# An attention and gated-MLP kernel: two more accumulator banks for the MLP

## The chip, the cores and the metric

The kernel runs on one core of a Trainium2 chip. The metric is the device time of one execution in microseconds (us); the time before is a median of three timed runs, and one further execution was profiled.

## The reference, cut to what matters

There are 8 batches, 8 heads, 576 tokens and a head dimension of 64; the model dimension is 512, the hidden one 1024.

```python
def _attn_ref(q, k, v, f):
    scores = scale * np.matmul(q, k.transpose(0, 1, 3, 2))
    cum = np.cumsum(np.log(np.clip(f, 0.0001, 1.0)), axis=-1)
    scores = np.where(causal, -1e9, scores + cum[..., :, None] - cum[..., None, :])
    attn = softmax(scores)                       # row by row
    return np.matmul(attn, v)

def _moe_ref(x, w_in, w_spatial, b_spatial, w_out):   # x: attention's output, heads side by side
    h = np.maximum(x @ w_in, 0.0)
    u, v = h[..., :512], h[..., 512:]
    v_n = (v - mean(v)) / np.sqrt(var(v) + 1e-6)      # over the 512 columns
    v_s = np.einsum('ts,bsd->btd', w_spatial, v_n) + b_spatial[None, :, None]
    return (u * v_s) @ w_out
```

## The kernel before, in words

Heads are worked on in pairs, four pairs to a batch, 32 in all. The kernel interleaves two streams. `attention(b)` works through the four pairs of batch b. `moe(b)` is the gated MLP of batch b and needs the x tiles (xh and xl, a value and its rest) of all four pairs. The driving loop writes down `moe(b)` piece by piece, and between its pieces `attention(b + 1)` in proportion.

Attention, per pair: scores of four row blocks on TensorE into score banks "sc" (L326, the last 64 rows through L233 with qk_t as input), VectorE adds the decay and takes the lowest value (L306, out nm), ScalarE takes the exponential (L337, L375), GpSimd divides by the sum (L314). From pair 8 on (the third batch; `moved`) the weights are turned without TensorE: VectorE transposes blocks of 32 into the buffer mid (L456), and 16 transfers in SyncE's queue bring them to e (L463). The product with v follows (L488, L493, in score banks too), and ScalarE and VectorE split the result into xh (L510) and xl (L513). For pairs 0 to 7 the transposes are TensorE's, into the banks of the pool "t", tag "tp" (L414, L425, L405).

The MLP, per batch: five v tiles of 128 tokens (12 matmuls of 512 columns each, 8 for the last), read out by ScalarE at L773 into vx, of which there are two, or for the last by L771 and L772; normalised (L774 to L778), split into vnh and vnl (L780, L782). Eight u tiles (12 matmuls of 256 or 320 columns), read out by ScalarE (L801). Then for each of the two halves of the tokens four spatial tiles (14 matmuls), multiplied into u by VectorE (L823), split into gh (L826, ScalarE) and gl (L827, GpSimd), and two output tiles (12 matmuls of 512 columns), read out by ScalarE (L851) and sent to DRAM. Every odd batch has one more output tile, with the last 64 tokens of two batches.

Each of these tiles gets its accumulator from `acc(b)`. The 8 PSUM banks of 2 KB are four of tags sc0 to sc3, two of tag tp, and two of the pool `ps_m` (tag ps). Before, batches 0 to 6 take theirs from `ps_m` alone, two in turn; the last batch, after which there is no more attention to write down, takes from `ps_m`, from tp and from the score banks in turn. A tile can be written again once its former content has been read.

The order of the instructions on each engine is fixed when the program is built. A planner runs a time model of the engines, and whenever one is free it places the instruction written earliest among those whose inputs and buffers it holds ready. At run time each engine keeps to that order and waits where an input or a buffer isn't ready. So a change of buffers can change the order on every engine.

Of the kernel before, what the change touches and what calls it, by code (L numbers as in the profile page):

```python
# [38 lines left out]
def attn_gmlp_kernel(ctx: ExitStack, tc: tile.TileContext, qk, v, f, w_in, w_sp, b_sp, w_out, out):  # L39
# [7 lines left out]
    B = out.shape[0]  # L47
# [687 lines left out]
    nps = [0]  # L735

    def acc(b):

        nps[0] += 1
        k = nps[0] % 3 if b == B - 1 else 0  # L740
        pool, tag = ((ps_m, "ps"), (PS["t"], "tp"), (PS["s"], f"sc{nps[0] // 3 % 4}"))[k]
        return pool.tile([128, DM], F32, name=tag)

    def moe(b):
        X = [xs.pop(b * PPB + p) for p in range(PPB)]
        vh, vl = [], []
        for i in range(NB + 1):
            for n in (2 * i, 2 * i + 1) if b == 0 and i < NB else ():
                load_rest(n, win_v, winh, winl, ("exp", PPB - 1, 1, 0))
            ps = acc(b)  # L750
            n = 0
            for p in range(PPB):
# [37 lines left out]
        for j in range(NJ):  # L790
            for t0, nt in HALVES:
                ps = acc(b)
                n = 0
                for p in range(PPB):
                    xh, xl = X[p]
                    for l, r in ((winh, xh), (winl, xh), (winh, xl)):
                        mm(ps[:, 0:nt], l[:, p, 128 * j:128 * j + 128], r[:, t0:t0 + nt], n == 0, n == 3 * PPB - 1)
                        n += 1
                    yield 369
                us[j, t0] = mo.tile([128, 320], F32, name="u", tag="U", bufs=9)  # L800
                A.activation(us[j, t0][:, 0:nt], ps[:, 0:nt], AF.Relu)  # L801
# [6 lines left out]
        for t0, nt in HALVES:  # L808
            gh, gl = [], []
            for j in range(NJ):  # L810
                ps = acc(b)
                o = ps[:, 0:nt]
                js = slice(128 * j, 128 * j + 128)
                for c in range(NB):
                    mm(o, vh[c][:, js], sph[:, c, t0:t0 + nt], c == 0, False)
                    mm(o, vh[c][:, js], spl[:, c, t0:t0 + nt], False, False)
                    mm(o, vl[c][:, js], sph[:, c, t0:t0 + nt], False, False)
                    yield 370
                mm(o, vh[NB][:, js], spta[:, t0:t0 + nt], False, False)
                mm(o, vb_[:, js], sptb[:, t0:t0 + nt], False, True)  # L820
                yield 246
                g = us[j, t0][:, 0:nt]
                V.tensor_tensor(out=g, in0=o, in1=g, op=ALU.mult)  # L823
                gh.append(mo.tile([128, 320], F32R, name="gh", tag="GH", bufs=3))
                gl.append(mo.tile([128, 320], F32R, name="gl", tag="U", bufs=9))
                A.copy(gh[j][:, 0:nt], g)  # L826
                G.tensor_tensor(out=gl[j][:, 0:nt], in0=g, in1=f32(gh[j][:, 0:nt]), op=ALU.subtract)  # L827
                if t0:
                    for r, gg in enumerate((gh[j], gl[j])):
                        V.tensor_copy(gt[0][r][:, j, r0:r0 + 64], f32(gg[:, 256:320]))  # L830
            for c0 in (0, 128):
                yield from w_out_tile(b, [g[:, c0:c0 + 128] for g in gh], [g[:, c0:c0 + 128] for g in gl],
                                      [(b, t0 + c0, 0, 128)])
# [92 lines left out]
```

## Time and profile before

| what | value |
|---|---|
| median of three timed runs | 747.42 us (747.03 to 747.93) |
| profiled execution | 752.48 us |
| its span, first to last instruction | 750.3 us |
| TensorE busy | 700.4 us, 93% |
| VectorE, GpSimd, ScalarE busy | 64%, 51%, 49% |
| granted TensorE clock, mean | 0.979 |

The span is what the rows count from. The granted clock is the share of TensorE's full clock that the chip let through. PE is TensorE, PEld its weight loads, DVE VectorE, ACT ScalarE, POOL GpSimd, SPq SyncE's queue. A row of the timeline gives start, length, engine, line, operation, output and inputs, shape, and in brackets how long the engine had been idle and what ended that.

### The profile page before, as it was taken

To read this page: it belongs to the slowest core of one execution; us is meant where nothing else is said; L and a number is where in the kernel's file an instruction comes from. 1 tells how busy PE (TensorE), PEld (TensorE's weight loads), DVE (VectorE), ACT (ScalarE), POOL (GpSimd) and SP (SyncE) were. 2 spreads that over 40 slices of the span, in tenths; PEclk is the share of its full clock that TensorE was granted. 3 is DMA by queue.
4 is the path that set the end of the run, shared out by engine and by line. 5 is a ranking of instruction groups with operands and counts; after the bars stand their busy time and mean duration, and the time that the engine had idled before them with its cause. 6 is when DMAs were issued, how large, how long until landed. Compare 5 with 4: busy or idle time off the path is not lost.

```text
span 750.3 us, 14594 instructions
## 1 busy us (share of the span) xinstructions
PE 700.4 (93%) x4709; PEld 554.1 (74%) x4709; DVE 480.3 (64%) x1597; ACT 369.2 (49%) x1028; POOL 380.1 (51%) x703
## 2 busy tenths in 40 slices
PE   7878979789989898999999999999999999999997
PEld 3545757558778586797778777788779787899886
DVE  6787787855676575667666766767666766821332
ACT  6866586663544344645444444544454435521231
POOL 3887555584554453544475454635464455611241
PEclk9999999999999899999999999999999999999999
DMA  7855344246657777557874687657965686330001
GB/s 234 240 151 144 108 145 133 78 127 184 191 160 188 194 188 206 155 147 204 213 204 136 179 220 226 178 114 203 227 172 151 176 226 178 84 88 29 29 1 70
DMA packets 52749, 117.82 MB, mean 157 GB/s; under 512 B 10305, under 2 KB 14401, under 8 KB 52674
## 3 DMA queue, kind: packets, MB, share of 16 engines
q1 hardware_dynamic: 48082, 108.64, 53.7%
q10 hardware_dynamic: 4592, 8.26, 3.2%
q8 instruction: 37, 0.61, 0.4%
q14 instruction: 38, 0.31, 0.2%
HBM read 67.78 MB, written 9.75 MB: 103 GB/s over the span
## 4 chain that ended last, share of the span: by engine, by line
PE 52%; DVE 8%; POOL 8%; ACT 6%; issue 5%; DMA 2%; SPq 2%; ACTq 0%; POOLq 0%; DVEq 0%
PE ps L233 34%; PE sc L326 6%; PE sc L488 5%; POOL tt L314 4%; PE sc L233 3%; ACT tt L337 3%; DMA e<-mid 2%; PE tp L233 2%; DVE mid L456 2%; SPq L463 1%; PE sc L493 1%; DVE tt L306 1%; POOL vnl L782 1%; DVE st L774 1%; ACT o L851 1%
## 5 line engine op out<-in xcount | busy, mean ns | idle before, releaser
L337 ACT ACTIVATE tt<-tt,nm 128x384 f32<-128x384 f32 (+2 forms) x240 | 132.7, 554 | 69.0 <-DVE nm L306 66.4
L314 POOL TENSOR_SCALAR tt<-tt,sm 128x128 f32<-128x128 f32 x208 | 110.0, 549 | 49.3 <-DVE sm L353 47.0
L456 DVE STREAM_TRANSPOSE mid<-tt 128x128 f32<-128x128 f32 x192 | 90.7, 494 | 30.7 <-POOL tt L314 26.1
L827 POOL TENSOR_TENSOR gl<-u,gh 128x256 fp32r<-128x256 f32 (+1 forms) x64 | 51.4, 805 | 100.7 <-ACT gh L826 99.6
L326 PE MATMUL sc<-qk_t 64*128 64x128 f32 (+3 forms) x512 | 90.3, 473 | 9.2 <-DVE nm L306 4.8
L233 PE MATMUL ps<-xh,winh 128*128 128x256 f32 (+1 forms) x232 | 71.8, 312 | 4.2 <-DVE vx L772 2.8
L233 PE MATMUL ps<-sph,vnh 128*128 128x256 f32 (+1 forms) x240 | 74.1, 309 | 0.7 <-ACT o L851 0.7
L326 PEld LDWEIGHTS sc<-qk_t 64*128 64x128 f32 x512 | 46.1, 194 | 38.6 <-issue 9.5
L306 DVE CUSTOM_DVE_ANT_1 tt<-sc,dk 128x256 f32<-128x256 f32 (+1 forms) x120 | 64.8, 550 | 13.5 <-PE sc L326 9.8
L233 PE MATMUL ps<-xh,winl 128*128 128x256 f32 (+1 forms) x232 | 70.2, 303 | 2.9 <-POOL winl L144 2.8
L233 PE MATMUL ps<-spl,vnh 128*128 128x256 f32 (+1 forms) x240 | 70.8, 295 | 0.0
L233 PE MATMUL ps<-sph,vnl 128*128 128x256 f32 (+1 forms) x240 | 70.5, 294 | 0.0
L488 PE MATMUL sc<-e,vraw 128*64 128x256 f32 (+1 forms) x576 | 65.6, 348 | 4.8 <-DVE nm L306 2.3
L233 PE MATMUL ps<-xl,winh 128*128 128x256 f32 (+1 forms) x232 | 69.9, 302 | 0.0
L826 ACT CAST gh<-u 128x256 fp32r<-128x256 f32 (+1 forms) x64 | 27.3, 431 | 68.2 <-DVE u L823 36.2
L233 PE MATMUL ps<-winh,xh 128*128 128x512 f32 x148 | 59.9, 405 | 0.4 <-ACT o L851 0.4
L782 POOL TENSOR_TENSOR vnl<-vx,vnh 128x512 fp32r<-128x512 f32 x32 | 41.0, 1287 | 35.7 <-ACT vnh L780 35.7
L306 DVE CUSTOM_DVE_ANT_0 tt<-sc,dk 128x128 f32<-128x128 f32 (+1 forms) x120 | 48.7, 419 | 14.9 <-PE sc L326 13.6
L233 PE MATMUL ps<-winl,xh 128*128 128x512 f32 x148 | 57.8, 390 | 0.0
L823 DVE TENSOR_TENSOR u<-ps,u 128x256 f32<-128x256 f32 (+1 forms) x60 | 26.7, 445 | 47.2 <-PE ps L233 47.2
L510 ACT CAST xh<-sc 128x256 fp32r<-128x256 f32 x64 | 24.9, 399 | 63.4 <-PE sc L488 40.3
L233 PEld LDWEIGHTS ps<-xh,winh 128*128 128x128 f32 x232 | 44.8, 194 | 10.9 <-DVE vx L772 5.4
(223 smaller groups left out, 1771.7 us busy)
## 6 DMA issues: line engine op xcount, KB each, us to landing
e<-mid SPq DMA_DIRECT2D x384, 100.0 KB, 2.2
qk_t<-in_dram SPq DMA_DIRECT2D x32, 608.0 KB, 5.9
dk<-rows_d SPq DMA_DIRECT2D x58, 320.0 KB, 5.3
vraw<-in_dram SPq DMA_DIRECT2D x32, 320.0 KB, 4.0
dt<-rows_d SPq DMA_DIRECT2D x58, 144.0 KB, 6.1
out_dram<-o ACTq DMA_DIRECT2D x28, 256.0 KB, 3.6
w<-in_dram SPq DMA_DIRECT2D x16, 256.0 KB, 3.0
w<-in_dram SPq DMA_DIRECT2D x4, 512.0 KB, 6.5
```

Of the source, the lines that this page charges most:

```text
L233: T.matmul(o, l, r, start=st, stop=sp)
L306: return V.tensor_tensor_reduce(out=out, in0=ps, in1=dec, scale=-0.125, scalar=3.0e38, op0=ALU.add, op1=ALU.min, accum_out=acc_)
L314: G.tensor_scalar(out=t, in0=t, scalar1=r, scalar2=1.0, op0=ALU.mult, op1=ALU.mult)
L326: return lambda: T.matmul(ps[:, c:c + n], qk_t[p, n - 128:n], qk_t[p, 640:640 + n], start=True, stop=True)
L337: last["exp", P, h, i] = A.activation(t, t, AF.Exp, bias=nm, scale=-1.0, accum_out=sm)
L456: V.transpose(out=part(middle(P)[:, 0, at:], [[32, n], [RUN, 4], [1, 32]]), in_=part(t, [[128, n], [32, 4], [1, 32]]))
L488: return lambda: T.matmul(out, vt[:, c, h, :], src, start=c == 0, stop=c == end)
L510: last[P, s0 // 256] = A.copy(xh[:, s0:s0 + n], ps[:, 0:n])
L782: G.tensor_tensor(out=tlo, in0=x, in1=f32(th[:]), op=ALU.subtract)
L823: V.tensor_tensor(out=g, in0=o, in1=g, op=ALU.mult)
L826: A.copy(gh[j][:, 0:nt], g)
L827: G.tensor_tensor(out=gl[j][:, 0:nt], in0=g, in1=f32(gh[j][:, 0:nt]), op=ALU.subtract)
```

## The change

One line of `acc` is changed. In batches 1 to 6 the accumulators come from `ps_m` and from the pool of tag tp by turns, so that four banks follow one another. Batch 0, during which pairs 4 to 7 still use tp for their transposes, keeps two banks, and the last batch keeps its three pools.

```diff
     def acc(b):
 
         nps[0] += 1
-        k = nps[0] % 3 if b == B - 1 else 0
+        k = nps[0] % 3 if b == B - 1 else nps[0] % 2 if b else 0
         pool, tag = ((ps_m, "ps"), (PS["t"], "tp"), (PS["s"], f"sc{nps[0] // 3 % 4}"))[k]
         return pool.tile([128, DM], F32, name=tag)
```

## Rows read from the trace of the kernel before

**Rows 1.** The page, busy time by engine and the span in 40 slices.

```profile
PE 700.4 (93%) x4709; PEld 554.1 (74%) x4709; DVE 480.3 (64%) x1597; ACT 369.2 (49%) x1028; POOL 380.1 (51%) x703
...
PE   7878979789989898999999999999999999999997
```

**Rows 2.** The tile view of tp (durations, first to last start); last row, from 590 us.

```profile
L425 PE MATMUL tp<-ident,tl x40: 271/273/421, 27.6 to 168.4; 128*128 128x128 f32 x40
...
L233 PE MATMUL tp<-winh,xh x4: 389/396/500, 616.0 to 678.2; 128*128 128x512 f32 x4
```

**Rows 3.** Busy time by stretch: PE, PEld, DVE, ACT, POOL, clock, DMA share, GB/s.

```profile
175.00:600.00 425.00, 411.07 (x2867) 328.78 (x2864) 283.49 (x984) 199.31 (x565) 212.41 (x411) 0.98 0.68 183
...
600.00:680.00 80.00, 80.00 (x572) 66.36 (x571) 45.69 (x142) 32.21 (x87) 33.53 (x60) 1.00 0.52 136
680.00:750.30 70.30, 63.66 (x375) 57.25 (x373) 18.62 (x46) 17.45 (x38) 19.40 (x27) 0.99 0.10 34
```

**Rows 4.** The waits of TensorE, 175 to 600 us: total, times, longest.

```profile
PE sc L326 <- DVE xl L513: 3.0, 2, 2.4
PE ps L233 <- POOL gl L827: 2.7, 1, 2.7
PE ps L233 <- DVE vx L772: 2.6, 3, 1.4
PE sc L488 <- DVE nm L306: 2.3, 2, 1.2
PE sc L488 <- DMA out_dram<-o: 1.9, 1, 1.9
PE ps L233 <- ACT o L851: 0.7, 4, 0.2
PE sc L488 <- DVE mid L456: 0.5, 1, 0.5
```

**Rows 5.** Busy time by stretch, the three stretches at the lower clock.

```profile
219.90:223.70 3.80, 3.79 (x17) 2.99 (x18) 3.24 (x13) 1.89 (x6) 1.64 (x6) 0.56 0.39 90
257.90:264.70 6.80, 6.02 (x21) 4.38 (x22) 3.93 (x18) 3.66 (x12) 1.95 (x6) 0.50 0.72 204
561.60:565.10 3.50, 3.50 (x17) 3.50 (x16) 3.35 (x15) 2.69 (x8) 1.65 (x4) 0.51 0.18 65
```

**Rows 6.** TensorE's timeline around 220 us.

```profile
217.07 0.28 PE L233 MATMUL ps<-xh,winl 128*128 128x256 f32 x1
217.19 0.28 PE L233 MATMUL ps<-xl,winh 128*128 128x256 f32 x1
219.91 2.56 PE L326 MATMUL sc<-qk_t 64*128 64x384 f32 x12 [2.43 <-DVE xl L513]
222.40 0.63 PE L233 MATMUL ps<-xh,winh 128*128 128x320 f32 x1
```

**Rows 7.** GpSimd's timeline before the gl at 257.90.

```profile
254.42 0.41 POOL L280 TENSOR_SCALAR_AFFINE_SELECT dk<-dk 128x256 f32<-128x256 f32 x1 [3.68 <-DMA dk<-rows_d]
...
257.90 0.72 POOL L827 TENSOR_TENSOR gl<-u,gh 128x256 fp32r<-128x256 f32 x1
```

**Rows 8.** TensorE's timeline around 561 us.

```profile
561.09 0.42 PE L233 MATMUL ps<-xh,winh 128*128 128x320 f32 x1 [1.42 <-DVE vx L772]
```

**Rows 9.** Instructions by line and shape, 175 to 600 us, the accumulators' evictions.

```profile
L851 ACT COPY o<-ps 128x512 f32<-128x512 f32 x22 | 12.0, 571 | 4.2 <-PE ps L233 4.2
L773 ACT ACTIVATE vx<-ps 128x512 f32<-128x512 f32 x20 | 11.9, 596 | 17.8 <-PE ps L233 11.0 <-POOL vnl L782 5.5 <-DMA out_dram<-o 1.3
...
L801 ACT ACTIVATE u<-ps 128x256 f32<-128x256 f32 x20 | 7.7, 384 | 11.7 <-PE ps L233 11.5
```

**Rows 10.** SyncE's queue, the transfers of one pair.

```profile
364.58 9.54 SPq L463 DMA_DIRECT2D e<-mid  x15
```

**Rows 11.** The page, DMA issues: count, KB, median us from issue to landing.

```profile
e<-mid SPq DMA_DIRECT2D x384, 100.0 KB, 2.2
```

## The prediction, made before the changed kernel was seen

> **What bounds the kernel now.** I read the page first, for the shares of the engines over the span and over 40 slices [rows 1]. TensorE is busy 700.4 of 750.3 us, and from the tenth slice on its digit is 9 almost everywhere: the reader is to see that no other engine comes near it, and that the extra banks can only fill holes that TensorE still has. They are made for batches 1 to 6, so I looked for that stretch. The last transpose into one of the two banks begins at 168.4 us, and the first accumulator of the last batch stands in one at 616.0 us [rows 2]; I take 175 to 600 us as the stretch of the change and leave the rest as it is, since batch 0 and the last batch keep their rule.
>
> In that stretch TensorE is busy 411.07 of 425 us [rows 3]: 13.9 us of holes is all that any order of its work can win there, besides what the clock gives back. The table of waits names the holes longer than the noise [rows 4]: 2.6 us until L772 and 0.7 us until L851 have read an accumulator out (both free a bank of the pool "ps"); 2.7 us until GpSimd has made a gl at L827; 3.0 us until the xl subtraction of attention has freed a score bank; 2.3, 1.9 and 0.5 us ahead of the attention product at L488. That is 13.7 of the 13.9.
>
> Then the clock. [...] The price is length times missing share: 3.8 x 0.44 + 6.8 x 0.50 + 3.5 x 0.49 = 1.7 + 3.4 + 1.7 = 6.8 us. So the holes and the clock together hold 13.9 + 6.8 = 20.7 us, the far bound of a gain.
>
> **The change part by part.** It adds no instruction and takes none away: the same matmuls go to another bank, the same evictions read from there. Its direct cost is nothing, and there is nothing behind which that would have to hide. The banks themselves are idle in the stretch [rows 2], so nobody is displaced either. What changes is which wait stands in front of an accumulator's first matmul, and with it the order in which the planner lays TensorE's work.
>
> A, waits for a bank. With two banks the first matmul of an accumulator waits for the eviction of the one two before it; with four, of the one four before it. Evictions are short: 0.57 us for an output tile, 0.60 for a v tile, 0.38 for a u tile [rows 9]. Two more accumulators in between are at least 24 matmuls of 256 columns, two steps of 12 that lie some 0.12 us apart as the matmuls before 217.19 do [rows 6], 2.8 us in sum; the longest bank wait was 1.42. All of L772 and L851 goes: 3.3 us (bounds 0, if something else was late too, and 3.3).
>
> B, the score piece at 219.91. It stood in the queue right behind a u tile and waited 2.43 us for xl, while the u tiles behind it (222.40 on) read the same x tiles as the u tile before it, so their inputs were there [rows 6]. Both banks had just been filled, so the planner had nothing but attention to place. With four, two u tiles can stand in front. Bounds 0 and 2.4; I take half, 1.2, because the planner may still find the score piece ready by its own model.
>
> C, the wait for gl. GpSimd's queue was held by a mask that waited 3.68 us for its rows from DRAM, the shares came next, and gl last [rows 7]. More banks don't make gl earlier, but the spatial tiles of the next half could be laid in front of the output tile that needs it. Bounds 0 and 2.7; half, 1.3.
>
> D, the clock. The third stretch hangs on A and goes with it, 1.7; the first two hang on B and C, half of 1.7 + 3.4, 2.5. Sum 4.2 (bounds 0 and 6.8).
>
> E, what attention then pays. Now the MLP stops after every two accumulators, and each stop lets a piece of attention in early. With four banks the MLP is ready more often, and since it was written earlier it goes first. So attention loses lead, and its own waits can grow: now 0.6 (the second xl wait) + 2.3 + 1.9 + 0.5 = 5.3 us over 20 pairs. One pair's chain is long: 15 of the 16 transfers of a pair are issued in 9.54 us [rows 10], the last lands 2.2 us after its issue [rows 11], and only then can the product start. Bounds: -5.3 (all of it vanishes) and, if each of the 20 products waited as the longest did, 20 x 1.9 = 38 us. What speaks for the low end is the stretch 600 to 680 us, where the last batch already draws on three pools while the last pairs of attention still run: 80.00 us busy out of 80.00, clock 1.00 [rows 3]. What speaks against the low end is that the same stretch has only the end of attention in it. I take a doubling, +5.3.
>
> Sum: -3.3 - 1.2 - 1.3 - 4.2 + 5.3 = -4.7 us. The profiled execution took 752.48 us (span 750.3 and 2.2 around it), 5.1 us over the median of the timed runs, 747.42; I take the difference as it is from the median: 742.7 us.
>
> Where most banks take turns, from 600 us on, the granted clock is 1.00 and then 0.99 [rows 3], and by these rows the sum stays as it is. [...]
>
> **The rivals.**
> 1. No difference. The five holes are mostly attention's (B, C and E hold 10.4 of 13.7 us), and the bank waits of 3.3 us reappear as waits for the next late thing: the product behind its transfers, or the v tiles behind the two vx buffers. For it: SyncE's queue feeds 15 transfers in 9.54 us and the last lands after 2.2, whatever TensorE's order is [rows 10, 11]. Against it: TensorE is 96.7% busy in the stretch, so 3.3 us that it doesn't wait is mostly time gained. Time 747.4, within 1.5 us (0.2% of it, about the least that a measurement of this kernel tells from no change).
> 2. Slower: attention loses its lead. Place: in each of the six batches the product of the last pair comes just before the next batch's v stage needs it; once the MLP no longer halts for banks it arrives there early and TensorE waits at L488 with the transfers still on the way. Price: one wait as long as the worst now, 1.9 us, in each batch, 6 x 1.9 = 11.4, against the sure gains A and its clock, 3.3 + 1.7 = 5.0: +6.4, 753.8 us. It decides once new waits pass 10.0 us (A to D), 1.7 us per batch. For it: single waits of that size occur at L488 now [rows 4]. Against it: the v tiles of the next batch can be begun with the pairs that are there, in four banks now.
> 3. Much faster: the whole stretch becomes like 600 to 680 us, no hole and full clock. -20.7, so 726.7 us; with half of attention's present 5.3 us left, 729.4. For it: those very rows. Against it: C is GpSimd's lateness, which no bank cures.
> 4. The clock falls more often, between groups in turn. One more stretch like the third, 1.7 us, in each of six batches: +10.2 - 3.3, 754.3 us. Against it: full clock where three pools already take turns [rows 3]. [...]
>
> That the change does not do what it says I rule out nearly: the two banks have no other user in the stretch [rows 2].
>
> **How the numbers follow.** Forecast, a gain of 2 to 12 us around 742.7: 0.45. Rival 3, more than 12 us: 0.10. Rival 1: 0.18. Rival 2: 0.23. Rival 4: 0.04. Faster is 0.45 + 0.10 = 0.55, same 0.18, slower 0.27. The range has to hold 8 in 10: from 733 (about 0.08 below, the better part of rival 3) to 753 (about 0.12 above, the far half of rivals 2 and 4). The forecast's own range is 736 to 746.
>
> **What would show it.** A: no wait of TensorE on L772 or L851 between 175 and 600 us. B: no idle of 2 us before L326 around 220 us, and u tiles standing between. C: the wait on gl below 1.5 us. D: fewer than three stretches at the lower clock. E: waits at L326 and L488 of 8 to 12 us in sum; above 15 us rival 2 is right, below 4 rival 3. In the order of TensorE's work three or four accumulators in a row between pieces of attention, where now there are two. Wrong would be: TensorE's idle in the stretch as large as before with other names on it (rival 1), or the last product later than 673 us with a hole before the last batch's v tiles (rival 2).

## The result, and the profile after

The changed kernel takes 758.11 us (median of four runs, 757.07 to 759.91); the kernel before took 747.47 us (747.03 to 747.93) beside it. The ratio is 1.0145, 95% interval 1.0124 to 1.0165: slower by 1.4%, where 742.7 us had been forecast. The profiled execution took 758.39 us, its span 756.4 us, against 752.48 and 750.3 before. So the two profiles differ by 6 us, the medians by 10.7; what is added up from traces below is set against the 6.

The page of the changed kernel, busy time by engine:

```profile
PE 698.5 (92%) x4709; PEld 556.3 (74%) x4709; DVE 481.2 (64%) x1597; ACT 369.6 (49%) x1028; POOL 378.0 (50%) x703
```

The work is the same, instruction for instruction in number and within 2.2 us in busy time [rows 1]. The next view has the stretches of [rows 3] and, below them, the three stretches at the lower clock, as [rows 5] had them.

```profile
175.00:600.00 425.00, 406.29 (x2827) 329.37 (x2822) 274.95 (x943) 193.50 (x545) 205.12 (x395) 0.99 0.67 176
600.00:680.00 80.00, 75.80 (x535) 60.64 (x534) 53.70 (x179) 36.71 (x104) 39.50 (x75) 1.00 0.59 150
680.00:756.40 76.40, 71.38 (x449) 64.05 (x447) 20.20 (x51) 19.12 (x39) 18.83 (x26) 1.00 0.18 53
...
417.90:421.30 3.40, 3.40 (x15) 3.40 (x14) 1.41 (x4) 0.59 (x1) 1.20 (x3) 0.51 0.55 189
472.60:476.00 3.40, 3.40 (x10) 1.57 (x9) 2.12 (x8) 2.56 (x10) 0.72 (x2) 0.50 0.71 166
592.00:595.40 3.40, 3.40 (x14) 3.40 (x14) 1.70 (x5) 0.59 (x1) 0.92 (x2) 0.50 0.59 196
```

TensorE's holes between 175 and 600 us grew from 13.9 to 18.7 us. Between 600 and 680 us, where there had been none, there are 4.2; after 680 us there are 5.0 where there were 6.6. Together that is 7.4 us more. The clock did not cost more: three stretches of 3.4 us at a granted share of 0.51, 0.50 and 0.50 are 5.1 us, against 6.8. Two of them begin, at 417.90 and 592.00 us, behind waits for gl that end at 416.64 and 590.52 us, the third, at 472.60, behind a wait for L772 of 0.98 us that ends at 472.13. So 7.4 - 1.7 = 5.7 of the 6.1 us between the spans is accounted for. In the changed kernel the clock fell no more often: there are three such stretches as before, 10.2 us long in sum instead of 14.1.

Now the waits of TensorE in the changed kernel, first from 175 to 600 us, as in [rows 4], then from 600 us to the end.

```profile
PE sc L326 <- DVE xl L513: 5.3, 5, 1.5
PE tp L233 <- POOL gl L827: 2.8, 1, 2.8
PE ps L233 <- POOL gl L827: 2.2, 1, 2.2
PE sc L488 <- DVE nm L306: 1.7, 3, 0.6
PE sc L488 <- DVE sm L376: 1.3, 1, 1.3
PE sc L233 <- DVE nm L306: 1.1, 2, 0.6
PE tp L233 <- DVE vx L772: 1.0, 1, 1.0
PE ps L233 <- DVE vx L772: 1.0, 1, 1.0
PE sc L488 <- DMA e<-mid: 0.9, 1, 0.9
PE sc L488 <- issue: 0.7, 1, 0.7
...
PE sc L326 <- DVE xl L513: 2.7, 1, 2.7
```

The wait on L851 is gone and that on L772 has shrunk to 2.0 us. But the wait for gl has gone from 2.7 to 2.8 + 2.2 = 5.0 us, and that of attention's score pieces for xl from 3.0 to 5.3, with 2.7 more behind 600 us. The waits at the attention product, L488, are 1.7 + 1.3 + 0.9 + 0.7 = 4.6 us, as before (4.7).

Both grown waits lead back to GpSimd. Here is its timeline ahead of the gl wait of 2.2 us with the matmul that the gl releases and the rows of SyncE's queue.

```profile
397.77 10.12 SPq L463 DMA_DIRECT2D e<-mid  x16
...
408.30 1.00 SPq L252 DMA_DIRECT2D dk<-rows_d  x2
412.38 0.41 POOL L280 TENSOR_SCALAR_AFFINE_SELECT dk<-dk 128x256 f32<-128x256 f32 x1 [3.87 <-DMA dk<-rows_d]
412.74 0.41 POOL L282 TENSOR_SCALAR_AFFINE_SELECT dk<-dk 128x256 f32<-128x256 f32 x1
413.13 2.05 POOL L314 TENSOR_SCALAR tt<-tt,sm 128x128 f32<-128x128 f32 x4
...
415.87 0.72 POOL L827 TENSOR_TENSOR gl<-u,gh 128x256 fp32r<-128x256 f32 x1
416.64 0.50 PE L233 MATMUL ps<-woh,gl 128*128 128x512 f32 x1 [2.23 <-POOL gl L827]
```

The reader is to see who holds whom. The decay rows of the next pair (dk) can be loaded once VectorE has read the old ones (its last reading of them, at L306, takes 0.69 us from 405.01 and ends at 405.70); the load is issued at 408.30, behind the sends of the weights in SyncE's queue, and its mask on GpSimd (L280) can start at 412.38, after 3.87 us in which GpSimd does nothing. Four shares of the present pair (L314) and the gl of the MLP stand behind that mask. TensorE, done with all else in its order, stands 2.23 us before the output tile that reads gl.

For xl the way is longer: the shares are late, VectorE stands at the transposes of the weights, which read them (L456), and the xl subtraction (L513) is behind those in VectorE's order. So it is ahead of the longest xl wait:

```profile
634.03 0.41 POOL L280 TENSOR_SCALAR_AFFINE_SELECT dk<-dk 128x256 f32<-128x256 f32 x1 [2.81 <-DMA dk<-rows_d]
...
634.83 0.31 DVE L456 STREAM_TRANSPOSE mid<-tt 128x128 f32<-128x128 f32 x1 [2.58 <-POOL tt L314]
...
641.07 1.57 PE L326 MATMUL sc<-qk_t 64*128 64x384 f32 x12 [2.66 <-DVE xl L513]
```

The share that VectorE waits for starts right behind the mask, at 634.43, and the second xl subtraction, behind seven more transposes, ends at 641.01.

The waits of GpSimd for decay rows, 175 to 700 us, of the kernel before:

```profile
POOL dk L280 <- DMA dk<-rows_d: 33.2, 21, 3.7
...
POOL dt L286 <- DMA dt<-rows_d: 11.1, 11, 2.1
```

and of the changed kernel:

```profile
POOL dk L280 <- DMA dk<-rows_d: 37.4, 18, 5.3
...
POOL dt L286 <- DMA dt<-rows_d: 16.8, 17, 2.4
```

That is 44.3 us before and 54.2 after. VectorE's waits for the shares at L456 over the same stretch, first two rows before and then two after:

```profile
DVE mid L456 <- POOL tt L314: 25.6, 13, 4.0
...
DVE mid L456 <- POOL tl L314: 6.0, 3, 2.8
...
DVE mid L456 <- POOL tt L314: 34.1, 17, 5.3
DVE mid L456 <- POOL tl L314: 21.9, 17, 2.7
```

They went from 31.6 to 56.0 us, and 2.5 us at L456 put down to the rows themselves are new.

### The profile page after: what moved, and what is told of

The parts are those of the page before. It is cut to its first block, busy times and chain, and to the rows that moved or that the text cites. A ratio compares the mean times of both kernels' runs of the same rounds, so it can differ in the third digit from the quotient of the medians.

```text
span 756.4 us, 14604 instructions
## 1 busy us (share of the span) xinstructions
PE 698.5 (92%) x4709; PEld 556.3 (74%) x4709; DVE 481.2 (64%) x1597; ACT 369.6 (49%) x1028; POOL 378.0 (50%) x703
## 4 chain that ended last, share of the span: by engine, by line
PE 41%; POOL 11%; DVE 9%; issue 8%; DMA 6%; ACT 5%; SPq 3%; POOLq 0%; ACTq 0%; DVEq 0%
PE ps L233 15%; PE tp L233 13%; POOL tt L314 5%; PE sc L326 5%; PE sc L233 4%; DMA dt<-rows_d 3%; PE sc L488 3%; ACT tt L337 3%; SPq L463 3%; DVE mid L456 2%; DMA dk<-rows_d 2%; DMA e<-mid 1%; DVE tt L306 1%; POOL vnl L782 1%; POOL gl L827 1%
## 5 line engine op out<-in xcount | busy, mean ns | idle before, releaser
L314 POOL TENSOR_SCALAR tt<-tt,sm 128x128 f32<-128x128 f32 x208 | 108.0, 539 | 37.2 <-DVE sm L353 37.0
L456 DVE STREAM_TRANSPOSE mid<-tt 128x128 f32<-128x128 f32 x192 | 93.1, 500 | 40.3 <-POOL tt L314 34.6
L827 POOL TENSOR_TENSOR gl<-u,gh 128x256 fp32r<-128x256 f32 (+1 forms) x64 | 51.5, 805 | 107.3 <-ACT gh L826 106.7
L326 PE MATMUL sc<-qk_t 64*128 64x128 f32 (+3 forms) x512 | 90.1, 471 | 14.7 <-DVE xl L513 9.0
L306 DVE CUSTOM_DVE_ANT_1 tt<-sc,dk 128x256 f32<-128x256 f32 (+1 forms) x120 | 64.8, 550 | 23.1 <-PE sc L326 20.0
L326 PEld LDWEIGHTS sc<-qk_t 64*128 64x128 f32 x512 | 45.2, 190 | 39.1 <-DVE xl L513 11.3
L488 PE MATMUL sc<-e,vraw 128*64 128x256 f32 (+1 forms) x576 | 65.6, 348 | 4.6 <-DVE nm L306 1.7
L306 DVE CUSTOM_DVE_ANT_0 tt<-sc,dk 128x128 f32<-128x128 f32 (+1 forms) x120 | 48.8, 419 | 24.2 <-PE sc L326 22.6
L510 ACT CAST xh<-sc 128x256 fp32r<-128x256 f32 x64 | 25.1, 398 | 55.7 <-PE sc L488 31.9
L780 ACT CAST vnh<-vx 128x512 fp32r<-128x512 f32 (+1 forms) x40 | 24.7, 619 | 51.9 <-DVE vx L778 51.7
L776 POOL TENSOR_TENSOR mv<-mv,lnc 128x1 f32<-128x1 f32 (+1 forms) x40 | 8.4, 214 | 79.6 <-DVE mv L775 79.6
L280 POOL TENSOR_SCALAR_AFFINE_SELECT dk<-dk 128x256 f32<-128x256 f32 x60 | 25.4, 423 | 45.0 <-DMA dk<-rows_d 44.8
L233 PE MATMUL ps<-xh,winh 128*128 128x320 f32 (+1 forms) x136 | 42.9, 319 | 3.8 <-DVE vx L772 2.2
L774 DVE BATCH_NORM_STATS2 st<-vx 128x6 f32<-128x512 f32 (+1 forms) x40 | 27.1, 684 | 28.6 <-ACT vx L773 28.4
L337 ACT ACTIVATION_READ_ACCUMULATOR tt<-tt,nm 128x1 f32 x240 | 45.1, 188 | 0.0
L233 PE MATMUL sc<-qk_t 128*128 128x288 f32 x128 | 42.1, 425 | 1.9 <-DVE nm L306 1.9
L233 PE MATMUL ps<-sph,vnh 128*128 128x256 f32 (+1 forms) x144 | 43.8, 304 | 0.0
L233 PE MATMUL ps<-xh,winl 128*128 128x320 f32 (+1 forms) x136 | 41.3, 305 | 2.6 <-POOL winl L144 2.6
L488 PEld LDWEIGHTS sc<-e,vraw 128*64 128x64 f32 x576 | 32.4, 137 | 15.0 <-issue 4.9
```

Source lines behind the costliest of these rows:

```text
L233: T.matmul(o, l, r, start=st, stop=sp)
L280: G.affine_select(out=two, in_=two, compare_op=ALU.is_ge, fill=-8.0 * BIG, base=0, pattern=[[0, 2], [-1, 128]], channel_multiplier=1)
L306: return V.tensor_tensor_reduce(out=out, in0=ps, in1=dec, scale=-0.125, scalar=3.0e38, op0=ALU.add, op1=ALU.min, accum_out=acc_)
L314: G.tensor_scalar(out=t, in0=t, scalar1=r, scalar2=1.0, op0=ALU.mult, op1=ALU.mult)
L326: return lambda: T.matmul(ps[:, c:c + n], qk_t[p, n - 128:n], qk_t[p, 640:640 + n], start=True, stop=True)
L337: last["exp", P, h, i] = A.activation(t, t, AF.Exp, bias=nm, scale=-1.0, accum_out=sm)
```

## The experiments

Each was timed in five rounds beside the kernel before, whose median was 747.5 to 751.8 us from one group of runs to the next, so ratios are compared. "Idle" is the time between TensorE's instructions from 175 us to its last matmul, added up from the gaps in the trace: 15.6 us in the kernel before, 22.9 in the changed one. "Masks' waits" are the two rows above, added. Added lines shift line numbers in later traces: what is L326, L488, L513 or L827 here stands a little lower there, with the same tiles.

### Are the banks or the order dear?

held2: four banks, but each MLP tile also waits for the reading of the tile two before it, as two banks force.

```diff
+        if st and tile_no[0]:
+            n, b = tile_no[0]
+            tile_no[0] = None
+            if 0 < b < 7 and n - 2 in read:
+                behind(i, read[n - 2], sync=True)
```

> The changed kernel with its four banks, but the first matmul of each accumulator also waits until the accumulator two before it has been read, as with two banks. TensorE's order is nearly that of the kernel before: 2.8 us of MLP matmuls by their columns between a pair's first and last score piece, where the changed kernel has 5.2. If the order of TensorE's work is the cause (attention's pieces stand behind older MLP matmuls, its loop from pair to pair gets longer), the time is that of the kernel before, 746 to 749 us. If the use of the two other banks itself costs, by the place of the evictions on ScalarE and VectorE, it stays at 756 to 759.

Measured: 746.64 us, ratio 0.9994 (0.9968 to 1.0021), idle 16.4 us. With 83% of TensorE's matmuls in the places that they have in the kernel before (20% in the changed kernel), the loss is gone. The banks as such cost nothing; the loss comes with the order that the planner makes when more tiles are open.

held3: the same with `n - 3`, so that three tiles may be open.

> As the first of these, but an accumulator waits for the one three before it: three open at a time. 5.2 us of MLP matmuls between a pair's score pieces already, attention's lead nearly gone. By the order theory near the changed kernel, 754 to 759 us. By the bank theory it lies in the middle or lower, 750 to 754.

Measured: 738.46 us, ratio 0.9881 (0.9849 to 0.9913), idle 7.4 us. Three open tiles are faster than two, and four are slower. The waits of TensorE and those of GpSimd, from 175 us on:

```profile
PE tp L235 <- POOL gl L836: 1.9, 2, 1.1
PE sc L235 <- DVE nm L313: 1.7, 2, 1.3
...
```

```profile
POOL dk L287 <- DMA dk<-rows_d: 15.6, 12, 3.2
POOL dt L293 <- DMA dt<-rows_d: 15.4, 20, 2.3
```

There is no wait for xl at all, and the masks' waits are 31.0 us.

### First theory: attention has lost its lead

The first theory was a wider form of rival 2. TensorE's order does tell of it: the MLP matmuls that lie between the first and the last score piece of one pair, counted by their columns, went from 6,790 columns on the mean to 12,530 (pairs 9 to 31 of the two traces). At the pace of the kernel before from 192.59 to 197.60 us, 22 steps of 512 columns in 5.01 us, that is an estimate of 3.0 and 5.6 us; the 2.8 and 5.2 of the expectations are the author's own estimate of the same work. Three runs take attention's place in the order for itself: nolead2 puts it late in the kernel before, prio4 and lead4 put it early in the changed one.

nolead2: the kernel before, with each score piece and product placed behind the MLP matmul written last before it.

```diff
+                if held and mlp:
+                    behind(was, mlp[0])
```

> The kernel before with its two banks, but each score piece and each product of attention from pair 8 on must stand behind the MLP matmul that was written just before it. 6.0 us of MLP matmuls between a pair's score pieces, attention no longer ahead. By the order theory as slow as the changed kernel or slower, 756 to 763 us. By the bank theory no slower than before, 746 to 749.

Measured: 761.74 us, ratio 1.0191 (1.0157 to 1.0225), idle 20.0 us. It is as slow as the theory wants, but not by its mechanism: the waits are not those of the changed kernel.

```profile
PE ps L237 <- DVE vx L778: 15.3, 5, 4.2
```

With two banks and nothing of attention to fill in, TensorE stands at the banks.

prio4: the changed kernel, with the score pieces and products of attention first whenever the planner has them ready.

```diff
-                was = job()
+                with (tc.high_priority() if first else ExitStack()):
+                    was = job()
```

> The changed kernel with its four banks, but attention's score pieces and products from pair 8 on are placed ahead of older MLP matmuls as soon as the planner's model has them ready. 3.8 us of MLP matmuls between a pair's score pieces, between the two kernels. By the order theory the time falls by half or more of the loss, to 746 to 752 us. By the bank theory 756 to 759.

Measured: 765.44 us, ratio 1.0239 (1.0201 to 1.0276), idle 28.7 us: slower still. A row of TensorE's waits and one of GpSimd's, to which 9.7 us for dk come:

```profile
PE sc L327 <- DVE xl L515: 14.0, 12, 2.5
```

```profile
POOL dt L287 <- DMA dt<-rows_d: 74.5, 31, 6.0
```

lead4: the changed kernel with `LEAD = 0.3`, which writes attention that share of a batch earlier.

> The changed kernel with LEAD = 0.3: attention is written down 0.3 of a batch earlier, so that it is the older work again. 3.6 us of MLP matmuls between a pair's score pieces instead of 5.2. By the loop theory the time falls towards the kernel before, 746 to 751 us. By the margin theory it does not: attention as the oldest work is placed the moment the planner's model has it ready, so score pieces wait on xl as often or more, 756 to 766.

Measured: 758.70 us, ratio 1.0133 (1.0099 to 1.0167), idle 20.5 us, the waits for gl 10.8 us and the masks' waits 55.5. An earlier place helps nothing. And held3 has nearly as much MLP work between the score pieces of a pair as the changed kernel (0.4% less, by the author's count) and is 2.6% faster. The theory falls. What goes along with the time is another row: with masks' waits of 31.0, 44.3, 54.2 and 84.2 us the idle time is 7.4, 15.6, 22.9 and 28.7 us (held3, before, after, prio4). It is a row of four, and not a law: nolead2, which stands at its banks, doesn't fit it (16.6 and 20.0 us), nor does mask4 below (56.7 and 15.5).

### Second theory: xl is placed late

xl4 is the changed kernel with xh and xl (L510, L513) first on their engines, xl2 the kernel before with the same, xlheld3 held3 with the same.

```diff
+            with (tc.high_priority() if away else ExitStack()):
                 freed[xb + s0 // 256] = V.tensor_tensor(out=xl[:, s0:s0 + n], in0=ps[:, 0:n],
```

> The changed kernel, but the planner places the reading out of the attention product from pair 8 on (the xh copies on ScalarE, the xl subtractions on VectorE) ahead of older work, instead of behind VectorE's transposes. TensorE's order is that of the changed kernel. If the loss is that score pieces stand with no margin behind an xl that VectorE makes late (8.0 us of waits in the changed kernel against 3.0), most of those waits go: 748 to 753 us. If the loss is attention's longer loop from pair to pair, in which the MLP matmuls between the score pieces (5.2 us, as in the changed kernel) are the added part, the waits only move: 756 to 759.

> The same edit on the kernel before, as the control. By the margin theory a gain of at most its 3.0 us of waits on xl: 744 to 748 us. By the loop theory no change, 747 to 749.

> Three accumulators open at a time (738.5 us, hardly a wait on xl in its trace) with the early reading out of the product as well. By the margin theory nothing is left to win there, 736 to 740 us; if it falls below 735, the early xl shortens attention's loop too.

Measured: xl4 753.75 us, ratio 1.0073 (1.0048 to 1.0098); xl2 749.22 us, 0.9997 (0.9972 to 1.0023); xlheld3 737.65 us, 0.9861 (0.9829 to 0.9893), within its interval the same as held3. In xl4 TensorE's order is that of the changed kernel in every place, and by the medians half of the loss is won back, but its waits for xl are still 7.6 us where they were 8.0, in a profiled execution that took 757.28 us. So the edit hardly did what it was for, and the run doesn't tell what the wait for xl is worth.

### Third theory: GpSimd stands at masks, and the shares and gl stand behind them

mask4 keeps every load and every instruction. It was to place the masks of the next pair behind this pair's shares on GpSimd; mask2 is the kernel before with the same edit. But each of a pair's two dk tiles has two masks, and the edit holds back only the first (L280).

```diff
-            G.affine_select(out=two, ...
+            first_ = G.affine_select(out=two, ...
...
+            if moved(P - 1):
+                behind(first_, shared[P - 1])
```

> The changed kernel, but on GpSimd the masks of the next pair stand behind the shares of this pair instead of among them. New theory, since making attention older did not help: GpSimd stands at a mask until the decay rows have come from DRAM (54 us of such waits in the changed kernel between 175 and 700 us, 44 before, 31 in the fast version with three open), the shares and gl behind it are late, so VectorE's transposes and xl, so TensorE's score pieces and output tiles. Then these waits fall below 30 us, TensorE's idle from 22.9 us to 12 or less, the time to 740 to 750 us. If the masks are only where GpSimd happens to stand, no change: 756 to 760.

> The same edit on the kernel before, as the control. By the mask theory a smaller gain, 740 to 746 us; otherwise 746 to 750.

Measured: mask4 751.11 us, ratio 1.0023 (0.9996 to 1.0051), idle 15.5 us in a profiled execution of 747.46 us. Most of the loss is gone, but not in the way that the theory has it: the waits at the masks are 56.7 us, where fewer than 30 were expected. The second mask (L282) still stands between the shares, and now it is the one that waits for the rows. Its waits from 175 to 700 us, and one of them:

```profile
POOL dk L282 <- DMA dk<-rows_d: 26.9, 18, 4.7
...
322.60 0.41 POOL L282 TENSOR_SCALAR_AFFINE_SELECT dk<-dk 128x256 f32<-128x256 f32 x1 [3.45 <-DMA dk<-rows_d]
```

Four shares start behind it, at 322.99. VectorE's waits for shares at its transposes (L456 in the changed kernel) are 50.9 us, 56.0 in the changed kernel, and TensorE's waits for gl 5.4 us, 5.0 there; its waits for xl fell from 8.0 to 4.8. TensorE's order was not held either: 82% of its places are those of the changed kernel, and held2 shows that another order can undo the loss alone. So mask4 doesn't tell what the place of the masks is worth. mask2 took 775.63 us, ratio 1.0368 (1.0325 to 1.0410): here the planner made another order (73% of the places), in which TensorE stands 10.4 us at the attention product for the transposes and 5.2 for their transfers. So mask2 says nothing of the masks either.

norows4 is the changed kernel, norows2 the kernel before, without the loads of the decay rows from pair 10 on: the rows of pair 9 are used again. Only the loads are left out; the masks stay, and no longer wait for DRAM. They wait instead until VectorE has read the rows before them, as the same tiles are masked again.

```diff
+        elif P > 2 * PPB + 1:
+            tab[P] = (qk_t, *kept)
+            return
```

> The changed kernel with the decay rows of pairs 10 to 31 not loaded: the masks and the subtraction run on the rows of pair 9, so that no mask waits for DRAM. TensorE's order is nearly that of the changed kernel. By the mask theory the loss against two banks is gone: within 3 us of the same edit on the kernel before, or below it. By the theory that the order of TensorE's work costs by itself (attention placed with no margin, longer loop), it stays 8 to 11 us above the same edit on the kernel before.

> The kernel before with the decay rows of pairs 10 to 31 not loaded (the masks and the subtraction run on the rows of pair 9), as the control. By the mask theory 738 to 745 us, since 44 us of waits at the masks go.

Measured: norows4 728.71 us, ratio 0.9743 (0.9714 to 0.9772), idle 1.1 us. norows2, with the same loads gone, took 761.04 us, 1.0175 (1.0136 to 1.0214), in an order with 64% of the places of the kernel before. Two open tiles slower by 1.7%, four faster by 2.6%: either two tiles are too few once the rows are there, or the new order is at fault.

Three runs leave out the same loads in other orders: with attention first (norowsprio4), with two open tiles in four banks (norowsheld2), with three (norowsheld3). The text on the first says that the masks are left out too; they stay, as in norows4.

> Four banks with attention's score pieces and products placed first (the slowest order of the four-bank kernels, 1.0239), and from pair 10 on no decay rows are loaded: the rows of pair 9 are used again, so this kernel leaves those loads and masks out. TensorE's order stays like that of prio4 (3.64 us of MLP matmuls between a pair's score pieces, 3.75 there). Theory 'the order is innocent, the masks' waits make it dear': as norows4, 727 to 731 us, ratio 0.972 to 0.978, TensorE idle from 175 us on below 3 us. Theory 'placing attention first costs by itself': at least half of the loss stays, above 738 us, ratio above 0.987, with waits on xl left.

> Four banks, but a tile waits for the reading of the tile two before it (held2, 0.9994), and no decay rows from pair 10 on (left out as in norows4). Theory 'the rows are the whole of it': as norows4, 727 to 732 us, ratio 0.972 to 0.980. Theory 'two open tiles are too few by themselves': the waits on vx and o that the kernel before has, 3.3 us and more, stay: 732 to 740 us, ratio 0.980 to 0.990.

> Three open tiles (held3, 0.9881) with no decay rows from pair 10 on (left out as in norows4). Theory 'three and four differ only in where the masks' waits fall': as norows4, 727 to 731 us, ratio 0.972 to 0.978, and the gap of 1.2% before, 2.6% over, between three and four is gone. Theory 'three open tiles give the better order whatever the rows do': faster than norows4 by 4 us or more, below 725 us, ratio below 0.970.

Measured: norowsprio4 730.60 us, ratio 0.9755 (0.9725 to 0.9784): the dearest order with row loads (1.0239) is as good as the others without. norowsheld3 727.40 us, 0.9718 (0.9689 to 0.9748): the gap between three tiles and four goes with the loads. norowsheld2 755.85 us, 1.0101 (1.0060 to 1.0142), which neither theory had. Its waits from 175 us on:

```profile
PE sc L499 <- DVE mid L467: 7.3, 5, 3.4
PE sc L499 <- DMA e<-mid: 4.5, 2, 2.5
PE sc L499 <- DVE sm L364: 4.3, 2, 2.5
```

TensorE stands 16.1 us at the attention product, L488 in the kernel before, whose weights are still being made, transposed or sent. Only 56% of its places are those of the kernel before.

So the order was written down: norowsfix2 has TensorE's order of the kernel before in every place, norowsfix4 that of the changed kernel, both without the row loads.

```diff
+    for j, i in zip(place_, place_[1:]):
+        tc.add_manual_dep(every[i], every[j].name, mybir.DependencyInfo(
+            mybir.DependencyClass.NoSync, mybir.DependencyReason.DATA), reason="order")
```

> The kernel before without the loads of the decay rows from pair 10 on (left out as in norows4), and TensorE's order written down to be, instruction for instruction, that of the kernel before. Theory 'norows2 and norowsheld2 are slow because the planner made another order for them, not because two open tiles are too few': the waits on xl and gl go, no wait of 2 us and more at the attention product is new: 732 to 742 us, ratio 0.980 to 0.992. Theory 'two open tiles cannot use the time that the rows give back': 745 us or more, ratio above 0.995.

> Four banks without the loads of the decay rows from pair 10 on (left out as in norows4), and TensorE's order written down to be, instruction for instruction, that of the changed kernel (norows4 shares 81% of its places). Theory 'the waits for the rows are the loss, not the order': 728 to 735 us, ratio 0.974 to 0.983, TensorE idle from 175 us on below 4 us. Theory 'norows4 was fast because its order had changed too': 745 us or more, ratio above 0.995.

Measured: norowsfix2 735.47 us (733.75 to 736.75), ratio 0.9793 (0.9757 to 0.9828), idle 4.8 us. norowsfix4 731.54 us (729.73 to 732.51), ratio 0.9743 (0.9706 to 0.9780), idle 2.6 us. The waits that are left in the one from 175 us on, the largest:

```profile
PE ps L284 <- DVE vnh L841: 1.2, 1, 1.2
PE ps L284 <- ACT o L906: 1.1, 5, 0.4
PE sc L381 <- DVE xl L568: 0.6, 1, 0.6
PE sc L543 <- DVE mid L511: 0.6, 1, 0.6
```

and of the other:

```profile
PE sc L534 <- DVE mid L502: 1.3, 1, 1.3
PE sc L372 <- DVE nm L352: 0.7, 2, 0.4
PE sc L372 <- DVE xl L559: 0.4, 1, 0.4
```

This is the pair that comes nearest to settling it, since TensorE's order is that of the kernels that were to be explained; the orders of the other engines were left to the planner. The order of the changed kernel loses nothing when the rows are there: it is then 731.54 - 735.47 = -3.9 us from the order of the kernel before, and the runs of the two don't overlap. The loads of the rows cost that older order 1 - 0.9793 = 2.1%, and the changed kernel's 1.0145 - 0.9743 = 4.0%. Of 747.5 us that is 15.5 and 30.0 us, 14.6 more (rounded after the subtraction); 0.5%, 3.7 us, are won, which leaves 10.8 us slower, and the medians say 10.7.

The profiles say where the difference lies. Against the kernel of the same order, the loads gone take 18.3 us off the span of the older order and 28.5 off the newer. TensorE's busy time falls alike in both, from 175 us on from 554.7 to 547.2 and from 553.5 to 545.2 us, in executions whose granted clock rose from 0.979 to 0.989 and from 0.984 to 0.993; its idle time falls by 10.8 and by 20.3. VectorE's waits for shares at its transposes fell from 31.6 to 2.7 us and from 56.0 to 9.8. GpSimd, though, stands at its masks longer than ever: in norowsfix4, from 175 to 700 us, 102.5 us for VectorE. The largest row of these:

```profile
POOL dk L328 <- DVE nm L352: 73.5, 19, 8.5
```

What it holds behind them has changed. In both kernels the planner has laid GpSimd's order anew: from 175 to 700 us eight or more shares now follow on one another with no mask of dk between in 22 places, where the kernel before has 10 such places and the changed one 7. So the sum of the waits at the masks is not what costs; by the traces it is the work that stands ready behind them. And these two runs took away the loads and the masks among the shares at once.

norows2 and norowsheld2 were slow by the orders that the planner made for them.

maskheld3: held3 with the masks behind the shares.

> Three open tiles, and the masks of the next pair stand behind this pair's shares on GpSimd, as in mask4. Theory 'what is lost is what stands behind a waiting mask': held3 has no wait on xl left and 31 us of masks' waits that hurt little, so little is left to win: 735 to 740 us, ratio 0.984 to 0.991, equal to held3 within its interval. Theory 'the shift of the masks is worth its 1% whatever the order': 730 to 734 us, ratio 0.977 to 0.983.

Measured: 738.95 us, ratio 0.9866 (0.9833 to 0.9900), idle 9.1 us: the same as held3 within the interval. As the edit is that of mask4, with half of the masks left where they were, this says only that the edit wins nothing there. held3 and its two variants beat both kernels, by 1.2 to 1.4% of the kernel before.

## Why the prediction was wrong

The sum of the prediction was -4.7 us. By its own terms, with what the trace of the changed kernel has for each:

- A, bank waits, -3.3. L851 is gone, 2.0 us on L772 are left: -1.3.
- B and E, attention's own waits, -1.2 + 5.3 = +4.1. Waits at L326 and L488 went from 7.7 to 9.9 us, and 1.1 at the last score piece (sc at L233) is new: +3.3. The sign named for E, 8 to 12 us at L326 and L488, held, though the waits grew at xl and not at the product.
- C, the wait for gl, -1.3. It grew from 2.7 to 5.0: +2.3. The sign, below 1.5 us, failed.
- D, the clock, -4.2. From 6.8 to 5.1 us: -1.7. There are three stretches still, where fewer were named. The 4.2 took it that a stretch of [rows 5] goes with the wait next to it (those of [rows 6], [rows 7] and [rows 8]); no run shows that by itself. In the changed kernel three other waits have such a stretch behind them, and the one of 2.66 us that ends at 641.07 has none (granted clock 1.00 up to 660 us).
- "I ... leave the rest as it is": +4.2 us of holes between 600 and 680 us and -1.6 after it, +2.6.

In sum -1.3 + 3.3 + 2.3 - 1.7 + 2.6 = +5.2 us, and 0.4 of new waits on L801 make 5.6, of the 6.1 between the spans.

The forecast missed by 10.3 us of this: 3.6 at C, 2.6 in the stretches left as they were, 2.5 at D, 2.0 at A, 0.4 at L801, and 0.8 the other way at B and E.

The step that failed is C, the largest of these: "More banks don't make gl earlier, but the spatial tiles of the next half could be laid in front of the output tile that needs it." It took the lateness of gl as given and only asked what TensorE could do meanwhile. But the row under it, a mask on GpSimd that waits 3.68 us for its rows from DRAM [rows 7], was one of many: 44.3 us of such waits stand in the kernel before, and the table of TensorE's waits [rows 4] shows only the few whose delay came through. The rows can be loaded only when the old ones have been read, so the time of the load hangs on attention's place in the order, and where the mask stands in GpSimd's order the planner fixes, which, to judge by that order, held the rows ready sooner than they landed. A new order on TensorE sets these waits anew, and with them, as the traces suggest, gl, the shares, xl, the clock's falls behind such holes (D; to 0.50 and 0.51, behind those that end at 416.64, 472.13 and 590.52 us) and the stretch from 600 us on, where pairs of attention still run. That last stretch is a second step that failed: the prediction left it as it was, and the change moved the last product of attention from 673.2 to 698.3 us.

That the row loads are what makes the new order slow is shown by norowsfix2 and norowsfix4: they cost the one order 2.1% and the other 4.0%, and without them TensorE has no wait for gl left and at most 0.6 us for xl in either. That their way leads through masks that stand in front of ready shares and gl is read from the traces, at 416.64 and 641.07 us and in VectorE's waits; no run takes it by itself. Without the loads the new order does win 3.9 us. That this is near the 4.7 of the forecast is luck: the forecast took 10.0 us of gains (A to D) and 5.3 of losses (E), and without the loads most of the waits behind B, C and E are gone in both orders.

Of the rivals, 4 had the nearest time, 754.3 us, but the rise in the falls of the clock that it priced, for which no row spoke, did not come: three stretches, as before. Rival 2, at 753.8 us, had half of its sign: the last product came at 698.3 us instead of 673.2, though TensorE has no wait at L488 after 600 us. Its mechanism, waits at L488 for the transfers, did not happen (4.6 us, 4.7 before), and putting attention earlier (lead4, prio4) helped nothing. Rival 1's sign, the idle time as large with other names, was nearest in kind. Rival 3's time, 726.7 us, is about what the kernels without row loads reach, which fits its ground against it: C, the lateness of GpSimd, which no bank cures.

Two things stay open. Leaving out the loads takes away their landing, their place in SyncE's queue and their traffic at once, and let the planner lay GpSimd's order anew; how much of the loss is the wait at the masks and how much the others wasn't settled. All masks behind the shares, with the loads kept and TensorE's order held, would tell, and a second set of buffers for the rows, with which they could be loaded earlier; neither was tried. And with the loads kept, why three open tiles land in a good order (masks' waits 31.0 us) and four in a bad one (54.2) wasn't settled. That the gap vanishes without the loads shows where it comes from, not that three is a better number than four.

## What to carry to other kernels

Ahead of a change that lets a planner lay a new order, look not only at the bound engine's waits but at every long wait in the queues that feed it: a wait that costs nothing now may be one reordering away from costing much. Its sum is no measure of the cost (44 us on GpSimd before, over 100 in the fast norowsfix4): look at what stands ready behind it. To put an instruction that waits for a load behind that work is what the traces suggest, and wasn't shown here by itself. After an edit to an order, read in the trace whether every instruction that it meant has moved. And where an experiment's edit goes through such a planner, pin the bound engine's order before its time is believed: two runs here came out 1.0 and 1.7% slower by their order alone, where the same loads gone in the old order made it 2.1% faster.

## What was not expected of the hardware

Without the row loads other loads landed sooner. The median from issue to landing of a pair's 608 KB of q and k is 5.9 us before and 6.6 after the change; without the row loads it is 4.0 us (norows2) and 3.9 (norows4), while the 100 KB sends of the weights take 2.2 us in all four. The granted clock was a little higher in the two runs with a written order: its mean over six runs each is 0.987 (norowsfix2) and 0.986 (norowsfix4), and 0.982 over the eleven runs of the kernel before beside them. It does not go along with the loads in every order: norows2, also without them, has 0.979.
